# Where a step's gathers of value blocks stand: ahead of a step, or behind the value products of the step before it

## The chip, the cores and the metric

The kernel runs on one core of one Trainium2 chip. The metric is the device time of one execution in microseconds. A core has TensorE (PE, matrix products; PEld is its loading of weights), VectorE (DVE), ScalarE (ACT), GpSimd (POOL) and SyncE (SP). Each takes its own queue of instructions in the order of the program and waits for the others through semaphores. SyncE only issues transfers here; GpSimd issues the gathers and also subtracts and copies.

## The reference

Two stages for 4 batches, 8 heads, 768 rows and a head width of 64. The first is attention with a block mask: of 24 blocks of 32 keys, a block of queries sees its neighbours, the first and the last block, and three blocks that are drawn at random; the first and the last block of queries see everything.

```
mask = |blk_i - blk_j| <= 1, or either block is the first or the last, or blk_j is sampled for blk_i
attn = softmax(where(mask, q @ k.T / 8, -1e9))        x = attn @ v, heads side by side (B, S, 512)
gate = sigmoid(sum over k of conv_w[k] * x shifted by 4 - k rows)
out  = (gate * (x @ w_val)) @ w_out
```

## The kernel before, in words

**Units and steps.** The blocks of queries are taken two at a time, as a pair: eleven pairs of inner blocks in each batch, and one global pair (first and last block) that counts as two units. `units` holds 52 units, four times 11 + 2. One step of the main loop, `for n in range(N + LAG_V)`, makes the scores of unit n, the value products of unit n - 2 (`LAG_V`) and the transposes of unit n - 1 (`LAG_T`). All work on an engine is chained in program order by `InOrder`, which is why nearly all rows of the profile carry line 83.

**The order within a step, before.** First come the loads: `more_keys()` and `more_values()` in turn until both are far enough ahead. Then scaling of queries, stores, a weight load, `scores` (names `sc`, `s`), the copies of key blocks to `kg` on GpSimd and ACT, `values` (name `av`), and then the transposes (`pt`) in two halves, with `fill` and `prepare` behind each half. `finish` (name `xp`) ends the step.

**Value blocks.** `load_values` fetches what a pair's value products need: on SyncE the two own blocks into `va`, on GpSimd two indirect gathers into `vb`, one for each block of queries. Both have three buffers, which come free when the value products of the pair three earlier are done. `more_values` lets the load for a pair go as soon as the value products that free its buffer have been put in the program, that is at the head of the following step. For the first pair of a batch it also puts the index arithmetic (`indices`) on DVE.

**The second stage.** It is worked off in between, by row tiles of 384 rows, two in a batch. `gates` is convolution and tanh on DVE and ACT (`th`). `split` makes a high part `xh` (ACT) and a low part `xl` (GpSimd, a subtraction). `project` is a generator of which each `fill` takes one call (the digits of `FILLS` tell how many fills a half makes, those of `STEPS` how many times `prepare` goes on). Its first four calls are groups of 12 products into `vp`; with each of them DVE makes `y` of the group before (two buffers), ACT its high part `yh`, and GpSimd, by `second`, its low part `yl` one call later. The next six calls are the halves of three output row blocks `op` of 128 rows, six products each. The first half of a block uses high parts only. The second half makes three low-part products, two high-part ones and one with the last low part; in the first block of a row tile that call, the sixth of ten, is also where the last `yl` is put in GpSimd's queue.

Of the kernel before, what the change touches and what calls it, by code (L numbers as in the profile page):

```python
# [22 lines left out]
CH = 4  # L23
KW = 5
TS = 384
TILES = [[(0, 384), (384, 384)]] * B
PAIRS = [(2 * p + 1, 2 * p + 2) for p in range(NP - 1)]
RING = 4
VRING = 3
# [3 lines left out]
LAG_T, LAG_V = 1, 2  # L33
# [13 lines left out]
FILLS = (  # L47
    "11111210010222221221011022"
    "22111000222222111202211111"
    "02021011111110020111111002"  # L50
    "11211111221001111120020111"
    "1200"
)
# [11 lines left out]
def attention_moe(ctx, tc, qb, kb, v, ve, sampled, w_val, conv_w, w_out, ident_in, slot_in, out):  # L65
# [142 lines left out]
    decoded = set()  # L208
# [25 lines left out]
    for b in range(B):  # L234
        bt = Batch()
# [198 lines left out]
    def values(un):  # L434
        pr = un.pr
        if un.e == 0:
            pr.av = ps_av.tile([128, 2, 2, DV], F32, tag="av", name="av")
        if pr.glob:
            for h in range(2):
                for c in range(6):  # L440
                    pt = un.PT[4 * h + c if c < 4 else 4 + 2 * h + c]
                    for hp in range(HP):
                        cols = slice(BLK * hp, BLK * hp + BLK)
                        hd = 2 * hp + h
                        matmul(
                            pr.av[cols, un.e, h, :], pt[:, cols], pr.bt.vn[:, c, hd * DV : (hd + 1) * DV],
                            start=c == 0, stop=c == 5, tile_position=(0, BLK * hp),
                        )
        else:
            slots = [(a, h, b, (4 * a + 2 * b + h) * DV) for a in range(2) for h in range(2) for b in range(2)]  # L450
            wide = pr.bt.b < WIDE
            if wide:
                for a, h, b, hd in slots:
                    matmul(
                        pr.av[64 * b : 64 * b + 64, a, h, :], un.PT[4 * h + 2 * a][:, 64 * b : 64 * b + 64],
                        pr.va[:, hd : hd + DV], start=a + h == 0, stop=False, tile_position=(0, 64 * b),
                    )
            for a, h, b, hd in slots:
                for c in range(1 if wide else 0, 2):
                    for j in range(2):  # L460
                        rows = slice(64 * b + BLK * j, 64 * b + BLK * j + BLK)
                        vt = pr.vb[:, j, :] if c else pr.va
                        matmul(
                            pr.av[rows, a, h, :], un.PT[4 * h + 2 * a + c][:, rows], vt[:, hd : hd + DV],
                            start=c == 0, stop=a + h == 2 if wide else c == 1, tile_position=(0, rows.start),
                        )
        if un.last:
            rs = three.tile([128, 2, 2, 2], F32, tag="rs", name="rs")
            dve.tensor_scalar_add(rs[:, 0], pr.av[:, :, :, D], 1e-9)
            dve.reciprocal(rs[:, 1], rs[:, 0])  # L470
            pr.x = two.tile([128, 2, 2, D], F32, tag="x", name="x")
            dve.tensor_tensor(
                out=pr.x, in0=pr.av[:, :, :, 0:D], in1=rs[:, 1, :, :, None].to_broadcast([128, 2, 2, D]), op=ALU.mult
            )
# [27 lines left out]
    def gates(m):  # L502

        xT, t, n = m.bt.xT, m.t, m.n
        m.th = two.tile([128, CH, TS], F32, tag="th", name="th")
        acc = [m.th[:, f, 0:n] for f in range(CH)]

        def first(f):
            act.activation(acc[f], xT[:, f, t : t + n], AF.Copy, scale=cw[:, f, 0:1])

        def tanh(f):
            act.activation(acc[f], acc[f], AF.Tanh, scale=0.5)

        first(0)
        yield
        for f in range(CH):
            for k in range(1, KW):
                dve.scalar_tensor_tensor(
                    out=acc[f], in0=xT[:, f, t + k : t + k + n], scalar=cw[:, f, k : k + 1], in1=acc[f],
                    op0=ALU.mult, op1=ALU.add,  # L520
                )
                if k == 1 and f + 1 < CH:
                    first(f + 1)
                if f and k == 2:
                    tanh(f - 1)
                yield
        yield
        tanh(CH - 1)
        m.bt.read.add(("gate", m.t))
        yield  # L530
# [89 lines left out]
    to_gate, to_split, to_project = [], [], []  # L620
# [6 lines left out]
    step = [0]  # L627

    def advance(jobs, after=None):

        m, g = jobs[0]
        try:
            next(g)
        except StopIteration:
            jobs.pop(0)
            if after is not None:
                after(m)

    def queue_rows(bt, t):
        m = Rows()  # L640
        m.bt, (m.t, m.n), m.ready, m.begun = bt, TILES[bt.b][t], [], False
        to_gate.append((m, gates(m)))
        to_split.append((m, split(m)))

# [5 lines left out]
    weights = load_weights()  # L650
    decoding = decode_weights()

    def fill(times=1):
        for _ in range(times):
            if "all" in decoded and to_project and step[0] > max(to_project[0][0].ready):
                advance(to_project)

    def prepare(steps):
        for _ in range(steps):
            if next(decoding, None):  # L660
                continue

            if to_gate and (to_gate[0][0].begun or len(gating) < 2):
                to_gate[0][0].begun = True
                gating.add(id(to_gate[0][0]))
                advance(to_gate, prepared)

        if {CH, CH + 1} <= decoded and len(staged) == 2 * CH and to_split and unread <= {id(to_split[0][0])}:
            advance(to_split, prepared)
# [5 lines left out]
    def freed(k):  # L675

        return units[min(k, N - 1)].pr.seq if k >= 0 else -1

    def more(which, upto, load):
        if at[which] < len(pairs) and pairs[at[which]].seq <= upto:  # L680
            load(pairs[at[which]])
            at[which] += 1
            return True

    def until(which, n, do):
        while at[which] < min(len(pairs), pairs.index(units[min(n, N - 1)].pr) + 1):
            do(pairs[at[which]])
            at[which] += 1
# [7 lines left out]
    for n in range(N + LAG_V):  # L696
        step[0] = n

        def more_keys():
            return more("keys", freed(n - 1) + RING, load_keys)  # L700

        def more_values():
            return more("values", freed(n - LAG_V - 1) + VRING, load_values)

        if n == 0:
            more_keys()
            numbers_first = {eng: list(block_numbers(pairs[0], eng)) for eng in (POOL, ACT)}
            until("scaled", 0, scale)
            indices(0)
            until("copied", 0, copy_keys)  # L710
            more_keys()
            until("copied", 1, copy_keys)
            more_values()
        else:
            while more_keys() or more_values():
                more_values()
        until("scaled", n + (SCALE_AHEAD if n else 1), scale)
        store()
        k = len(staged)
        if k < 2 * CH and n >= WEIGHTS_AT[k] and (k < 4 or k - 4 in decoded):  # L720
            next(weights)

        if n < N:
            scores(units[n])
        if n == 0:
            more_keys()
        until("copied", n + COPY_AHEAD, copy_keys)
        if n == 0:
            while more_keys() or more_values():
                more_values()  # L730
        if 0 <= n - LAG_V < N:
            values(units[n - LAG_V])
        if 0 <= n - LAG_T < N:
            for half, _ in enumerate(transposes(units[n - LAG_T])):
                at_half = 2 * n + min(half, 1)
                fill(int(FILLS[at_half]))
                prepare(int(STEPS[at_half]))
        else:
            fill(1)
            prepare(int(STEPS[2 * n]))  # L740
        if 0 <= n - LAG_V < N and units[n - LAG_V].last:
            pr = units[n - LAG_V].pr
            finish(pr)
            pr.bt.done.add(pr.p)
            for t, (r0, rn) in enumerate(TILES[pr.bt.b]):
                need = {p for p in range(NP - 1) if any(r0 <= i * BLK < r0 + rn for i in PAIRS[p])}
                if r0 == 0 or r0 + rn == S:
                    need.add(-1)
                if t not in pr.bt.queued and need <= pr.bt.done:
                    pr.bt.queued.add(t)  # L750
                    queue_rows(pr.bt, t)
# [53 lines left out]
```

## Time and profile before

| | before |
|---|---|
| median of 3 runs | 403.19 us |
| the runs | 397.3, 403.19, 405.37 us |
| span of the profiled execution, first to last instruction | 371.7 us |
| what lies around it, by the runs shown | 25.6 to 33.7 us |
| TensorE busy | 347.2 us, 93% of the span |
| DVE, ACT, GpSimd busy | 256.9, 253.9, 221.4 us |
| gathers into vb | 88 |

Of the profiled execution the page gives the span and no time of its own; the runs give whole times. Times of the trace count from the start of the span. In the rows, the first number of a timeline is the start, the second the length, xN the number of instructions merged, and the brackets give the idle time of the engine ahead of the row and what ended it.

### The profile page before, as it was taken

The numbers are of one execution on the slowest core, as the hardware profiler recorded it, in microseconds if no ns is written. First come the engines' busy times: TensorE is split into PE (matmuls) and PEld (weight loads), VectorE is DVE, ScalarE is ACT, GpSimd is POOL, SyncE is SP. The second block draws the span as 40 slices with busy tenths as digits, with TensorE's granted clock in tenths as the row PEclk, the third lists the DMA queues.
The fourth block names the chain that finished last, engine by engine and source line by source line (L and its number), as shares of the span: only waits on it lengthen the run. The fifth ranks groups of instructions, "written<-read, shape, count | busy, mean of one in ns | idle before, by whom it ended". The sixth has DMA issues, their size and how long they took to land.

```text
span 371.7 us, 15536 instructions
## 1 busy us (share of the span) xinstructions
PE 347.2 (93%) x6274; PEld 274.2 (74%) x6274; DVE 256.9 (69%) x546; ACT 253.9 (68%) x619; POOL 221.4 (60%) x309
## 2 busy tenths in 40 slices
PE   8889789798969999999999999999999999999895
PEld 7456456565646887797779877888888788888794
DVE  4465659975796779577977867586479848959420
ACT  2887678896788777766677587667667766755221
POOL 1888564988478658655861476658454744525540
PEclk9999989998989999999999999999999999999999
DMA  6999983899984537889798257788862473010202
GB/s 231 301 322 318 324 258 91 281 262 297 342 234 113 151 79 222 243 241 280 185 305 260 71 146 234 208 272 260 247 202 83 134 204 109 21 68 19 82 6 86
DMA packets 52585, 72.37 MB, mean 195 GB/s; under 512 B 6944, under 2 KB 34720, under 8 KB 52512
## 3 DMA queue, kind: packets, MB, share of 16 engines
q1 hardware_dynamic: 44896, 47.69, 42.5%
q0 software_dynamic: 7040, 23.43, 21.0%
q8 instruction: 50, 0.82, 0.9%
q10 hardware_dynamic: 576, 0.24, 0.2%
q14 instruction: 23, 0.19, 0.2%
HBM read 65.05 MB, written 6.29 MB: 192 GB/s over the span
## 4 chain that ended last, share of the span: by engine, by line
PE 71%; DVE 10%; DMA 6%; issue 4%; POOL 4%; ACT 4%; SPq 0%; ACTq 0%; POOLq 0%; DVEq 0%
PE op L83 15%; PE vp L83 15%; PE av L83 13%; PE pt L83 12%; PE sc L83 10%; DVE mx L83 4%; DMA vb<-in_v,idx 4%; PE xp L83 3%; PE s L83 3%; DVE th L83 2%; DMA k<-in_k 2%; ACT ptr L83 1%; POOL yl L83 1%; POOL vb L83 1%; DVE words L83 1%
## 5 line engine op out<-in xcount | busy, mean ns | idle before, releaser
L83 POOL DMA_INDIRECT vb<-in_v,idx x88 | 88.5, 1006 | 48.5 <-PE av L83 24.9
L83 DVE SCALAR_TENSOR_TENSOR th<-xT,cw,th 128x384 f32<-128x384 f32 x128 | 100.8, 796 | 11.8 <-ACT th L83 9.5
L83 ACT ACTIVATE pe<-sc,mx 128x256 f32<-128x256 f32 x176 | 69.2, 479 | 39.0 <-DVE mx L83 38.9
L83 DVE TENSOR_REDUCE mx<-sc 128x2 f32<-128x512 f32 x88 | 56.6, 685 | 42.1 <-PE sc L83 39.7
L83 POOL TENSOR_TENSOR yl<-y,yh 128x384 fp32r<-128x384 f32 x32 | 35.9, 1121 | 59.7 <-ACT yh L83 54.5
L83 ACT COPY ptr<-pt 128x512 f32<-128x512 f32 x112 | 65.1, 603 | 7.7 <-PE pt L83 7.5
L83 POOL COPY kg<-k 128x256 f32<-128x256 f32 (+1 forms) x143 | 51.0, 394 | 8.3 <-DMA k<-in_k 8.2
L83 PE MATMUL sc<-kg,qc 64*32 64x256 f32 x1408 | 52.5, 396 | 2.0 <-ACT pe L83 1.4
L83 PE MATMUL op<-wo,yh 128*128 128x512 f32 x192 | 53.6, 401 | 0.0
L83 PE MATMUL pt<-ident,pe 128*128 128x128 f32 x352 | 52.2, 283 | 0.0
L83 PE MATMUL vp<-xh,wv 128*128 128x384 f32 x256 | 51.3, 341 | 0.0
L83 PEld LDWEIGHTS av<-va,ptr 128*32 128x32 f32 (+1 forms) x1056 | 31.0, 118 | 22.3 <-issue 10.9
L83 PEld LDWEIGHTS pt<-ident,pe 128*128 128x128 f32 x352 | 39.5, 142 | 6.8 <-issue 0.4
L83 PEld LDWEIGHTS vp<-xh,wv 128*128 128x128 f32 x256 | 44.2, 188 | 0.2
L83 PE MATMUL av<-va,ptr 128*32 128x65 f32 (+1 forms) x1056 | 40.4, 226 | 3.2 <-ACT ptr L83 3.1
L83 POOL TENSOR_TENSOR xl<-xT,xh 128x384 fp32r<-128x384 f32 x32 | 36.6, 1149 | 11.0 <-ACT xh L83 10.9
L83 PE MATMUL av<-vb,ptr 128*32 128x65 f32 x1408 | 38.4, 222 | 1.6 <-DMA vb<-in_v,idx 1.4
L83 PEld LDWEIGHTS op<-wo,yh 128*128 128x128 f32 x192 | 34.7, 188 | 6.6
L83 PEld LDWEIGHTS sc<-kg,qc 64*32 64x32 f32 x1408 | 22.9, 109 | 18.3 <-issue 8.2
L83 PE MATMUL op<-wo,yl 128*128 128x512 f32 x96 | 31.8, 412 | 1.6 <-POOL yl L83 1.5
L83 PEld LDWEIGHTS av<-vb,ptr 128*32 128x32 f32 x1408 | 30.2, 110 | 3.6 <-DMA vb<-in_v,idx 2.1
L83 DVE SCALAR_TENSOR_TENSOR y<-th,vp 128x384 f32<-128x384 f32 x32 | 17.6, 549 | 20.6 <-PE vp L83 18.7
(72 smaller groups left out, 453.2 us busy)
## 6 DMA issues: line engine op xcount, KB each, us to landing
kg<-in_k SPq DMA_DIRECT2D x165, 64.0 KB
vn<-in_v SPq DMA_DIRECT2D x12, 520.0 KB
qc<-in_q SPq DMA_DIRECT2D x48, 128.0 KB
k<-in_k SPq DMA_DIRECT2D x12, 512.0 KB
out<-ot SPq DMA_DIRECT2D x23, 256.0 KB
va<-in_v SPq DMA_DIRECT2D x44, 130.0 KB
wst<-in_w_val SPq DMA_DIRECT2D x4, 512.0 KB
wst<-in_w_out SPq DMA_DIRECT2D x4, 512.0 KB
```

The costliest lines, as they stand in the source:

```text
L83: made = getattr(self.eng, name)(*args, **kwargs)
```

## The change

The load of a pair's value blocks is allowed one place earlier: in step n, directly behind the value products that free the buffer, instead of at the head of step n + 1. There is one exception. Where the first half's fills would make a row tile's sixth call, the one with the last low-part products of its first block, the load stays behind that half (behind its fills and its `prepare`). `groups` counts the calls that a row tile has made.

```
+    def may_project():
+        return "all" in decoded and to_project and step[0] > max(to_project[0][0].ready)
+
     def fill(times=1):
         for _ in range(times):
-            if "all" in decoded and to_project and step[0] > max(to_project[0][0].ready):
+            if may_project():
+                to_project[0][0].groups += 1
                 advance(to_project)
+
+    def before_last_low(times):
+
+        return may_project() and to_project[0][0].groups <= CH + 1 < to_project[0][0].groups + times
...
         if 0 <= n - LAG_V < N:
             values(units[n - LAG_V])
+
+        def next_values():
+            while more("values", freed(n - LAG_V) + VRING, load_values):
+                pass
+
+        if n >= LAG_V and not before_last_low(int(FILLS[min(2 * n, len(FILLS) - 1)])):
+            next_values()
         if 0 <= n - LAG_T < N:
             for half, _ in enumerate(transposes(units[n - LAG_T])):
                 at_half = 2 * n + min(half, 1)
                 fill(int(FILLS[at_half]))
                 prepare(int(STEPS[at_half]))
+                if n >= LAG_V:
+                    next_values()
```

`CH` is 4, so `CH + 1` is the number of the sixth call, counted from 0. In `queue_rows` a row tile now starts with `groups` at 0.

## Rows read from the trace of the kernel before

**Rows 1.** Busy time by stage: stretch in us and its length, then busy time and number of instructions for PE, PEld, DVE, ACT and POOL, the granted TensorE clock, the DMA share and GB/s.

```profile
50.00:110.00 60.00, 50.08 (x1195) 35.23 (x1180) 47.88 (x103) 49.08 (x129) 43.97 (x71) 0.96 0.84 247
110.00:331.00 221.00, 220.03 (x4207) 178.79 (x4206) 164.18 (x331) 156.72 (x368) 132.71 (x163) 0.99 0.62 184
```

**Rows 2.** The list of waits: who waited for whom, us in total, times, longest.

```profile
PEld op L83 <- POOL yl L83: 3.2, 4, 1.8
...
PE av L83 <- DMA vb<-in_v,idx: 1.4, 2, 0.9
```

**Rows 3.** Timeline of GpSimd, 56 to 78 us.

```profile
64.22 1.27 POOL L83 TENSOR_TENSOR wv<-words,wv 128x512 fp32r<-128x512 f32 x1 [4.74 <-ACT wv L83]
65.64 0.99 POOL L83 DMA_INDIRECT vb<-in_v,idx  x1
...
75.03 1.27 POOL L83 TENSOR_TENSOR wo<-words,wo 128x512 fp32r<-128x512 f32 x1
76.46 1.02 POOL L83 DMA_INDIRECT vb<-in_v,idx  x1 [0.16 <-PE pt L83]
```

**Rows 4.** The chain of work that ended last, in order of time: start, length in us, what.

```profile
77.78 6.77 DMA vb<-in_v,idx
...
218.46 1.07 PE av L83 x64
```

**Rows 5.** Timeline of TensorE, 79 to 89 us (steps 14 to 16).

```profile
79.35 1.09 PE L83 MATMUL pt<-ident,pe 128*128 128x128 f32 x8
...
80.79 1.12 PE L83 MATMUL sc<-kg,qc 64*32 64x256 f32 x32
...
82.85 0.57 PE L83 MATMUL av<-va,ptr 128*64 128x65 f32 x12 [0.67 <-ACT ptr L83]
...
84.60 0.66 PE L83 MATMUL av<-vb,ptr 128*32 128x65 f32 x30 [0.95 <-DMA vb<-in_v,idx]
...
85.19 1.97 PE L83 MATMUL pt<-ident,pe 128*128 128x128 f32 x8
...
87.51 1.61 PE L83 MATMUL sc<-kg,qc 64*32 64x256 f32 x32
```

**Rows 6.** Busy time in short stretches, columns as in rows 1.

```profile
81.80:85.20 3.40, 1.78 (x57) 1.27 (x49) 1.29 (x2) 3.24 (x10) 3.23 (x7) 1.00 1.05 322
85.20:88.60 3.40, 3.40 (x38) 2.65 (x42) 1.95 (x6) 1.76 (x4) 3.10 (x6) 0.50 1.09 288
...
341.20:344.60 3.40, 2.45 (x11) 1.69 (x9) 3.37 (x5) 2.23 (x6) 3.40 (x3) 1.00 0.01 2
```

**Rows 7.** Timeline of step 24: GpSimd, and the last output product of the call on TensorE.

```profile
137.33 1.13 POOL L83 DMA_INDIRECT vb<-in_v,idx  x1
...
140.42 1.00 POOL L83 TENSOR_TENSOR yl<-y,yh 128x384 fp32r<-128x384 f32 x1
...
141.48 0.50 PE L83 MATMUL op<-wo,yl 128*128 128x512 f32 x1 [0.20 <-POOL yl L83]
```

**Rows 8.** Timeline of TensorE in step 35: the last value products, then the two calls of output products.

```profile
212.74 0.32 PE L83 MATMUL av<-vb,ptr 128*32 128x65 f32 x8
...
213.40 1.63 PE L83 MATMUL op<-wo,yh 128*128 128x512 f32 x6
...
215.22 0.95 PE L83 MATMUL op<-wo,yl 128*128 128x512 f32 x3
...
216.72 0.50 PE L83 MATMUL op<-wo,yl 128*128 128x512 f32 x1
```

**Rows 9.** Timeline of GpSimd in step 35 and at the head of step 36.

```profile
211.34 1.01 POOL L83 TENSOR_TENSOR yl<-y,yh 128x384 fp32r<-128x384 f32 x1 [4.52 <-ACT yh L83]
212.30 1.01 POOL L83 TENSOR_TENSOR xl<-xT,xh 128x384 fp32r<-128x384 f32 x1
215.37 1.29 POOL L83 TENSOR_TENSOR yl<-y,yh 128x384 fp32r<-128x384 f32 x1 [2.07 <-ACT yh L83]
...
218.11 0.99 POOL L83 DMA_INDIRECT vb<-in_v,idx  x1 [0.16 <-issue]
219.41 0.95 POOL L83 DMA_INDIRECT vb<-in_v,idx  x1 [0.30 <-issue]
```

**Rows 10.** Timeline around 165 us: the last value products of step 28 on TensorE, and the first gather behind them on GpSimd.

```profile
164.59 0.32 PE L83 MATMUL av<-vb,ptr 128*32 128x65 f32 x8
...
165.25 0.99 POOL L83 DMA_INDIRECT vb<-in_v,idx  x1 [2.46 <-PE av L83]
```

**Rows 11.** Timeline of step 40: a yl on GpSimd, the last value products on TensorE, and the y on DVE that takes the buffer which this yl reads.

```profile
241.18 1.01 POOL L83 TENSOR_TENSOR yl<-y,yh 128x384 fp32r<-128x384 f32 x1
...
242.35 0.32 PE L83 MATMUL av<-vb,ptr 128*32 128x65 f32 x8
...
245.46 0.55 DVE L83 SCALAR_TENSOR_TENSOR y<-th,vp 128x384 f32<-128x384 f32 x1 [1.20 <-PE vp L83]
```

**Rows 12.** Timeline: one scaling of a query block on DVE, the load of a query block on SyncE, and the scaling of that block on DVE.

```profile
217.01 1.10 DVE L83 TENSOR_SCALAR qc<-qc 128x256 f32<-128x256 f32 x1
...
232.03 0.38 SPq L83 DMA_DIRECT2D qc<-in_q  x1
...
238.42 0.29 DVE L83 TENSOR_SCALAR qc<-qc 128x256 f32<-128x256 f32 x1
```

**Rows 13.** All gathers: duration on GpSimd in ns (shortest, median, longest), first and last start in us, number.

```profile
L83 POOL DMA_INDIRECT vb<-in_v,idx x88: 942/966/1317, 12.3 to 313.5; - x88
```

More of the change, by code (lines that the diff above doesn't have):

```diff
@@ L640, in queue_rows @@
         m = Rows()
-        m.bt, (m.t, m.n), m.ready, m.begun = bt, TILES[bt.b][t], [], False
+        m.bt, (m.t, m.n), m.ready, m.begun, m.groups = bt, TILES[bt.b][t], [], False, 0
         to_gate.append((m, gates(m)))
```

## The prediction

> **What bounds the kernel now.** I read the busy time by stages first [rows 1]. From 110 to 331 us TensorE is busy 220.03 of 221 us, so there is no more than about 1 us to gain there, while whatever makes TensorE wait is lost in full. Before that, from 50 to 110 us, it is busy 50.08 of 60 us: this is where earlier gathers could pay. The list of waits comes next [rows 2]: TensorE waits for gathered value blocks 1.4 us in all, and its weight loads wait 3.2 us for yl. So the worth of the change to TensorE is small on either side. Then I went along the GpSimd queue step by step (a step begins with its scores; V is the end of its value products) and looked for places where a gather is late, or where yl is only just in time.
>
> **The change, part by part.** It adds and removes no operation. The two gathers that stood at the head of step n+1, with the load of va on SyncE and three times a run the index arithmetic on DVE, move to behind the value products of step n. What they are moved past: on GpSimd the yl and xl subtractions of step n, on SyncE the stores and key loads of step n+1, on DVE the gate work of step n. The new wait is GpSimd's and SyncE's wait for V, earlier in their queues; behind it are those subtractions, for which TensorE waits, and those loads.
>
> *Gathers that come too late now.* At 84.60 us TensorE waits 0.95 us for a gather [rows 5]; the chain of waits leads to the transfer that began at 77.78 and took 6.77 us [rows 4]. Its pair stood in the GpSimd queue behind a weight subtraction at 75.03, and the whole queue was late, because GpSimd had idled 4.74 us ahead of 64.22 for ACT [rows 3]. After the change the pair of 65.64 (2.25 us by the pair in [rows 9]) goes into that idle time, and the pair of 76.46 also passes its 1.27 us subtraction: some 3.5 us earlier, against 0.95 wanted. **-0.95**; the other end is 0, if the transfer lands no earlier because the DMA engines are full there (share 1.05 and 1.09) [rows 6].
>
> *The clock behind that wait.* TensorE idled 0.67 and 0.95 us [rows 5] in a stretch where it was busy 1.78 of 3.4 us, and in the next stretch its granted clock is 0.50, the 1.2 GHz level [rows 6]. There 8 transposes take 1.97 us and the scores 1.61, where they took 1.09 and 1.12 a step before at full clock [rows 5]: 0.88 + 0.49, and about 0.2 for the two small transposes between them, is 1.6 us. Without the 0.95 the stretch would be busy 2.7 of 3.4 us, more than the 2.45 in the tail where the clock stayed at 1.00 [rows 6]. I take **-1.6**; the other end is 0, if the clock falls a little later instead.
>
> *Step 24 (TensorE at 137 to 144 us).* A gather at 137.33 stood ahead of yl at 140.42, and the last low-part product began at 141.48 after 0.20 us idle [rows 7]. The gathers go to step 23. Step 24 is one that the new test protects, so its own new gathers stay behind this yl. **-0.2**, between 0 and the whole 0.2.
>
> *Step 35 (TensorE at 211 to 217 us).* Here the two fills of the step are one call in each half: the first half makes the call of six high products (213.40), the second the call of three low, two high and one low product (215.22 to 216.72) [rows 8]. The test looks at the first half alone, finds no such call there and lets the gathers go ahead. V is 212.74 + 0.32 = 213.06. Where a gather waits for value products alone it begins 0.3 us after them (164.59 + 0.32, then 165.25) [rows 10], which gives 213.4. Two gathers with their gap take 219.41 + 0.95 - 218.11 = 2.25 us [rows 9], to 215.6. Only then come the yl that ran at 211.34 (1.01, to 216.6), the xl that ran at 212.30 (1.01, to 217.6) and the last yl, now at 215.37 (1.29; 1.01 at its best, to 218.65) [rows 9]. The third low product wants the first of these at about 215.7, the last product the second at 216.72 [rows 8]. So TensorE idles about 0.9 us, makes its two high products, and idles some 1.2 us more; the last product starts at 218.65 and not at 216.72: **+1.95**. Nothing covers it, since all that TensorE has next is behind this product. From below +1.0, if the xl is not ahead of the last yl in time; from above +2.2, with the 1.29.
>
> *The clock behind that.* About 2.1 us idle within 3 us is more than the 1.62 ahead of the fall at 85; the tail's 0.95 of 3.4 lowered nothing [rows 5, 6]. By the nearer row, the first, it falls: **+1.6**, the price from above; other end 0.
>
> *The other row tiles.* In four of them a yl at an early fill gets behind V and two gathers. Step 40: the yl of 241.18 moves to 242.35 + 0.32 + 0.3 + 2.25 = 245.2, ends at 246.2, and DVE's y at 245.46, which reuses the buffer that this yl reads, waits until then: 0.8 us [rows 11]. Behind it on DVE are gate sums; TensorE still has 12 projection products, four transposes, 6 output products and the next scores before it wants the next maxima. I take 0; upper end 0.8 us for each of four, were DVE's lateness passed on in full.
>
> *SyncE.* The load of va now waits for V ahead of the next step's query and key loads, where these waited for the end of the scores: later by a step's value products, 1.07 us [rows 4]. The shortest time from a query load to the scaling that needs it is 232.03 to 238.42 [rows 12], 6.4 us, and keys are loaded three steps ahead of their scores. **0**; a late query would stop DVE for the excess, once, 1 us at most. The index arithmetic, on 24 columns, is smaller than the 0.29 us of the scaling of 256 [rows 12], and delays DVE's gate work by that: 0.
>
> *The ports.* DVE's scaling of a query took 1.10 us at 217.01, beside a GpSimd subtraction, and 0.29 at 238.42 [rows 12]: the two engines can hold each other up. All 88 gathers lie between 942 and 1317 ns [rows 13], so a gather costs at most 0.35 us more by it, and I take 0. The Trainium skill (SBUF — State Buffer, Who interferes with whom) says that the second of DVE and GpSimd to ask for their common ports is fully blocked until the first is done; the same page gives about 3100 ns for a GpSimd-issued DMA beside a DVE copy, 620 ns alone. An estimate from that page would make step 35 some 4 us longer; the trace of before has no gather like it.
>
> **Sum:** -0.95 - 1.6 - 0.2 + 1.95 + 1.6 = +0.8 us. Of its execution the profile gives the span alone, 371.7 us; the runs shown have 397.3 to 405.37 with a median of 403.19, so 25.6 to 33.7 us lie around the span, and nothing in the change touches them. Forecast: 403.2 + 0.8 = **404.0 us**. That is no change: 2%, or 8 us, is about what a measurement of this kernel can tell from none.
>
> **Rivals.** (a) *Slower:* the early gain does not come, because the full DMA engines land the gathers no earlier, and step 35 loses its 3.55: 406.7. If also DVE passes on 0.8 us in four row tiles, 409.9. It decides whether in step 35 the last yl ends after 216.72, and whether DMA at 75 to 88 us is bound by its load rather than by the issue. For it: TensorE has no slack after 110 us [rows 1], and the DMA share [rows 6]. Against it: GpSimd idles 4.74 us ahead of 64.22, so the gathers can go out before the full stretch [rows 3]. (b) *Faster:* the early 2.75 are gained (with step 24), and step 35 loses 1.0 without a fall of the clock: 401.4; if it lost nothing, 400.4. For it: the clock did not fall in the tail [rows 6]. Against: GpSimd takes its queue in the program's order. (c) *The move does nothing:* GpSimd waits for V anyhow, as ahead of 165.25 [rows 10], so that the gathers start where they did: 403.2. Against: the pair of 218.11 starts 5 us behind its V [rows 8, 9]. (d) *The ports:* gathers beside DVE's work take longer at step 35 by 0.35 us each and hold up DVE too: +0.7, 404.7. By the page of the Trainium skill named above it would be about 408.
>
> **How the numbers follow.** Forecast 404.0: 0.55. (a) 406.7: 0.15, its far end 409.9: 0.05. (b) 0.15. (c) 0.07. (d) 0.03. The range reaches from (b)'s 400.4, less 2 us for the spread of the runs, to (a)'s 406.7 and the 2.2 us by which the highest run lies above the median: 398 to 409. Faster by over 2% means below 395.1; no case gives that, and I leave it 0.04 for runs like the 397.3 on top of (b). Slower by over 2% means above 411.3: (a)'s far end with a slow run, 0.08. Within 2%: 0.88.
>
> **What would show it.** Right: no wait for a gathered block at step 15 and a granted clock of 1.00 there; gathers 0.3 us behind V wherever GpSimd is free; in step 35 yl behind two gathers, TensorE idle ahead of its third low and its last low product; no such wait in steps 24, 30 and 41. Wrong: step 35 without that idle time (the forecast is then too high by up to 3.55), a fall of the clock elsewhere, DVE's y waiting for yl with TensorE idle behind late maxima, or a query load that DVE waits for.

## The result, and the profile after

| | before | after |
|---|---|---|
| median | 404.28 us (4 runs, 397.3 to 407.31) | 384.95 us (4 runs, 384.27 to 385.59) |
| ratio of the times | 1 | 0.9644, 95% interval 0.9592 to 0.9696 |
| span of the profiled execution | 371.7 us | 383.8 us |
| time of that execution less its span | not given | 385.59 - 383.8 = 1.8 us |

The change made the kernel 3.0 to 4.1% faster; the forecast was no change. The two records say the opposite of the times: the span after is 12 us *longer* than the one shown of before. That is the riddle of this case, and its solution is that the record of before and its times belong to different conditions. The same kernel before ran at 401 to 406 us in four sittings and at 373 to 376 us in five (a sitting is a set of runs made together on one chip), never in between; within a sitting all its runs stay at one level, apart from one of 1780.98 us. Medians are of all runs, ratios of the fast runs alone, those within 1.5% of the fastest of their kernel. The record shown of before, with a span of 371.7 us, is one of the lower level; its times are of the upper.

The page of after and its list of waits (who waited for whom: us in total, times, longest):

```profile
span 383.8 us, 15523 instructions
...
PE 350.1 (91%) x6274; PEld 275.0 (72%) x6274; DVE 264.1 (69%) x546; ACT 253.6 (66%) x619; POOL 221.0 (58%) x309
```

```profile
PE av L83 <- issue: 4.6, 9, 1.0
PE op L83 <- POOL yl L83: 3.3, 3, 1.3
...
PE s L83 <- ACT xT L83: 1.9, 2, 1.7
```

The wait for gathered blocks of [rows 2] is no longer in the list. A record of this kind could not name it, as it gives no landing time for gathers (see the last section), but the list of r3, which is of the lower level, has none either. TensorE's waits for yl have grown from 1.5 us to 3.3: 2.00 us of them belong to step 35, which came out as forecast, the rest to the tail, which has them in before too. New are waits put down to "issue" inside the value products, of which the list that [rows 2] is taken from has none. TensorE in step 35, after (rows 8 answer to it):

```profile
220.17 0.72 PE L83 MATMUL op<-wo,yl 128*128 128x512 f32 x2
221.95 0.50 PE L83 MATMUL op<-wo,yl 128*128 128x512 f32 x1 [1.06 <-POOL yl L83]
222.29 0.63 PE L83 MATMUL op<-wo,yh 128*128 128x512 f32 x2
223.85 0.50 PE L83 MATMUL op<-wo,yl 128*128 128x512 f32 x1 [0.94 <-POOL yl L83]
```

GpSimd in the same step (rows 9 answer to it):

```profile
219.64 1.23 POOL L83 DMA_INDIRECT vb<-in_v,idx  x1 [0.30 <-issue]
220.90 1.00 POOL L83 TENSOR_TENSOR yl<-y,yh 128x384 fp32r<-128x384 f32 x1
221.84 1.01 POOL L83 TENSOR_TENSOR xl<-xT,xh 128x384 fp32r<-128x384 f32 x1
222.81 0.98 POOL L83 TENSOR_TENSOR yl<-y,yh 128x384 fp32r<-128x384 f32 x1
```

The gather, then yl, xl and the last yl: TensorE waits for the first yl and the last one. And the clock behind it (stretch, length, busy time of PE, PEld, DVE, ACT, POOL, granted clock, DMA share, GB/s):

```profile
224.33:227.74 3.41, 3.41 (x83) 1.92 (x82) 2.36 (x4) 1.56 (x4) 1.52 (x3) 0.50 0.18 53
```

### The profile page after: what moved, and what is told of

Read it like the earlier page. It is cut to its first block, busy times and chain, and to the rows that moved or that the text cites. A ratio compares the mean times of both kernels' runs of the same rounds, so it can differ in the third digit from the quotient of the medians.

```text
span 383.8 us, 15523 instructions
## 1 busy us (share of the span) xinstructions
PE 350.1 (91%) x6274; PEld 275.0 (72%) x6274; DVE 264.1 (69%) x546; ACT 253.6 (66%) x619; POOL 221.0 (58%) x309
## 4 chain that ended last, share of the span: by engine, by line
PE 65%; DVE 16%; ACT 7%; issue 6%; POOL 3%; DMA 1%; ACTq 1%; DVEq 0%
PE av L83 13%; PE op L83 13%; PE vp L83 13%; PE sc L83 11%; PE pt L83 9%; DVE th L83 7%; DVE mx L83 4%; PE xp L83 3%; PE s L83 3%; ACT pe L83 2%; ACT ptr L83 1%; DVE x L83 1%; POOL vb L83 1%; DMA sb<-in_sampled 1%; ACT kg L83 1%
## 5 line engine op out<-in xcount | busy, mean ns | idle before, releaser
L83 POOL DMA_INDIRECT vb<-in_v,idx x88 | 89.7, 1019 | 91.4 <-PE av L83 66.1
L83 DVE SCALAR_TENSOR_TENSOR th<-xT,cw,th 128x384 f32<-128x384 f32 x128 | 111.0, 875 | 11.8 <-ACT th L83 9.5
L83 POOL TENSOR_TENSOR yl<-y,yh 128x384 fp32r<-128x384 f32 x32 | 34.7, 1091 | 38.6 <-ACT yh L83 38.2
L83 POOL COPY kg<-k 128x256 f32<-128x256 f32 (+1 forms) x143 | 52.2, 402 | 8.1 <-DMA k<-in_k 8.0
L83 PE MATMUL av<-va,ptr 128*32 128x65 f32 (+1 forms) x1056 | 41.3, 229 | 4.5 <-ACT ptr L83 2.2
L83 PE MATMUL av<-vb,ptr 128*32 128x65 f32 x1408 | 40.0, 225 | 2.6 <-issue 2.4
L83 POOL TENSOR_TENSOR xl<-xT,xh 128x384 fp32r<-128x384 f32 x32 | 35.4, 1111 | 6.1 <-ACT xh L83 5.9
L83 PEld LDWEIGHTS av<-vb,ptr 128*32 128x32 f32 x1408 | 31.1, 112 | 4.8 <-issue 3.2
```

What stands on the lines that cost most here:

```text
L83: made = getattr(self.eng, name)(*args, **kwargs)
```

## The experiments

**Is the profiled execution of before a typical one? (r1)** The kernel before, unchanged.

> The kernel before, unchanged. In the changed kernel's runs the whole time is 1.8 us above the span (385.59 against 383.8); in the kernel before, the median of 404.28 is 32.6 us above the profiled span of 371.7. Theory A: the profiled execution of the kernel before was an unusually quick one, and its usual executions have a span about 2 us below their time, near 402 us; then this run shows a span of 395 to 406 us, a time 1 to 3 us above it, and in the trace waits of 20 us or more that the first profile does not have. Theory B: the span is 372 us in every execution and 30 us lie around it; then this run shows a span of 370 to 374 us and a time of 397 to 407 us.

374.15 us (372.47 to 377.29), beside 374.04 for its twin; span 371.2, so 1.8 us lie around it. On this chip it simply ran 30 us faster than in the first runs. The "25.6 to 33.7 us around the span" of the prediction do not exist.

**The step that the test misses (r2).** The exception looks at both halves of a step, and holds the gathers back behind the first half if the second makes the sixth call:

```
-        if n >= LAG_V and not before_last_low(int(FILLS[min(2 * n, len(FILLS) - 1)])):
+        if n >= LAG_V and not before_last_low(sum(int(x) for x in FILLS[2 * n : 2 * n + 2])):
...
-                if n >= LAG_V:
+                if n >= LAG_V and not (half == 0 and before_last_low(int(FILLS[2 * n + 1]))):
```

> The changed kernel, with the exception made for both halves of a step: only step 35's GpSimd queue differs from it (two gathers go behind two yl and two xl). If the idle 2.0 us at step 35 and the fall of the clock behind it are what the changed kernel loses there, this run shows no idle time at step 35, a granted clock of 1.00 in steps 36 and 37, and a time 3 to 4 us below the changed kernel's 384.95: 381 to 382 us. Rival: the lost time comes back elsewhere, since the gathers of step 35 then land later; the time stays within 1 us of 384.95.

377.03 against 374.04, ratio 1.0122 (1.0057 to 1.0187). Step 35 has no idle time and a clock of 1.00; from the start of step 35 to that of step 38 it takes 17.86 us (before 17.34, after 21.04). So the mechanism of step 35 is as predicted, and undoing it does not bring the time below that of before. The times of the expectation miss, as this sitting was at the other level.

**The change again, and its two halves apart (r3 to r5).** `load_values` split into the own rows (SyncE, va) and the gathered rows (GpSimd, vb); r4 moves the gathers alone, r5 the own rows alone.

> The changed kernel, unchanged, beside new runs of the kernel before. The kernel before took 404 us in the first set of runs and 374 in the second, with a span 1.8 us below its time in both the profile (371.7) and the second set. Theory A: where the kernel before takes 374, the change costs time (the changed kernel with step 35 protected took 377.03 there), and this run is 378 to 382 us, a loss of 4 to 8; its gain in the first set comes from a condition in which the kernel before is slow. Theory B: the change gains the same 4% everywhere, which would be 358 to 362 us beside 374, with step 35's loss offset by something the two first profiles don't show.

377.87 against 375.93, ratio 1.0061 (1.0025 to 1.0098): on this chip, where before needs 376, the changed kernel is about 2 us *slower*.

> Only the gathers on GpSimd (with their index arithmetic) go behind the value products, as in the changed kernel; the loads of va on SyncE stay at the head of the next step, as in the kernel before. If GpSimd's queue is what the change is about, gain or loss, this run is within 1 us of the changed kernel. If SyncE's earlier wait (va ahead of the key loads) costs something, this run is quicker than the changed kernel by that, 1 to 3 us.

381.26, ratio 1.0162 (1.0088 to 1.0236); TensorE waits once for 3.0 us for va.

> The other part alone: the loads of va on SyncE go behind the value products, the gathers stay at the head of the next step. If GpSimd's queue is what matters, this run is within 1 us of the kernel before, with no idle time at step 35. If SyncE's order matters, it moves by the 1 to 3 us that the gathers alone do not show.

380.12, ratio 1.0162 (1.0069 to 1.0255); TensorE waits three times, 3.8 us in all, for gathered blocks. Neither part gains where before is at its lower level. Both miss their expectations: they are 3.4 and 2.3 us above r3, and why a part costs more than the whole is open.

**Another chip (r6 to r8).** The change, the wider exception of r2, and the change without any exception (`if n >= LAG_V:`).

> The changed kernel once more, in a third set, beside the kernel before. Theory A (the gain of the first set belongs to a condition in which the kernel before runs at 397 to 407 us): the result depends on what the kernel before takes in this set; at 372 to 378 the changed kernel is 0 to 6 us slower, at about 400 it is quicker and at 380 to 386. Theory B (it is always quicker): 358 to 362 us beside 374.

384.73, and before beside it 403.78 (402.89 to 406.54): ratio 0.9526 (0.9481 to 0.9571). This is the first result again.

> The changed kernel with the exception made for both halves of a step, now beside the changed kernel itself. From the traces, TensorE's way from the scores of step 35 to those of step 38 took 21.05 us in the changed kernel and 17.86 with this protection: if nothing hides that, this run is 2 to 4 us quicker than the changed kernel. Rival: it is not, because the spread of the stage before 120 us (2 to 4 us from execution to execution) covers it.

384.85, ratio 0.9508 (0.9448 to 0.9568): no difference from r6 that can be measured, and not the 2 to 4 us expected. The records say why: in r7 step 35 has no idle time, but the gathers held back (223.82 and 225.12 us) run beside the value products of step 36, which take 3.39 us instead of 1.14, and in r6 the idle time of step 35 had no fall of the clock behind it. Steps 35 to 38 take 19.52 us in r7 and 19.50 in r6.

> The changed kernel without its exception: in steps 24, 30 and 41 too, the gathers go ahead of the last yl. By the working of step 35, each of the three loses about 2 us of idle time at the last low-part product, and 1.5 us more where the clock falls behind it: 6 to 10 us slower than the changed kernel. Rival: yl was early enough in these steps, and the exception is worth nothing (within 1 us).

395.15, ratio 0.9774 (0.9717 to 0.983), 10.4 us more than r6. Steps 24, 30 and 41 now have what step 35 has, with 1.88 to 1.89 us idle in each; TensorE at step 24:

```profile
148.77 0.60 PE L83 MATMUL op<-wo,yl 128*128 128x512 f32 x1 [1.88 <-POOL yl L83]
```

and its clock is 0.50 in 149.03 to 152.44. The exception is worth its place: half of the gain hangs on it.

**The kernel before recorded at the upper level, and which part carries the gain there (r9 to r11).** r9 is before, r10 as r4, r11 as r5.

> The kernel before, unchanged, to see it recorded on a chip where it needs about 404. What is to be read is where the some 30 us lie that it needs less on the two other chips, and whether they stand behind waits of the value products for gathered or own rows (tags vb and va). Theory G (gathers that land late: before starts each gather a half step later than changed, and the smallest time from landing to first use was 0.1 to 2 us around steps 13 to 18): on a chip with 404 the record shows TensorE's value products waiting on vb at several places, together some 5 to 15 us, each followed by about 3.4 us at a granted clock of 0.5. Theory P (something that has nothing to do with the values: waits for a transposed or scaled tile, or for instructions): the vb and va waits stay under 2 us in all, and the idle time stands elsewhere. On a chip where before needs about 374 the record is as before's: vb waits under 2 us, and the question stays open.

402.12; span 399.3. Waits of TensorE in this record:

```profile
PE av L83 <- issue: 13.0, 33, 1.1
PE xp L83 <- DVE x L83: 8.5, 6, 2.6
```

and in r1, the same program at the lower level:

```profile
PE xp L83 <- DVE x L83: 1.5, 3, 0.7
...
PE av L83 <- issue: 0.8, 1, 0.8
```

> Only the gathers start early; the own rows' loads stay where the kernel before has them. On a chip where before needs about 404: theory G says 385 to 390, as the whole change; theory P in the form that the own rows' loads on SyncE carry the gain says 400 or more. On a chip where before needs about 374: 378 to 381 as in the first run of it.

386.38, ratio 0.9667 (0.9566 to 0.9768).

> Only the own rows' loads start early; the gathers stay where the kernel before has them. On a chip where before needs about 404: theory G says 398 to 406, no gain that can be told; if the own rows' loads carry the gain it says 385 to 390. On a chip where before needs about 374: 377 to 381 as in the first run of it.

405.34, ratio 1.0145 (1.0076 to 1.0213). The gathers carry all of the gain, the own rows none. Theory G was right in that, and wrong in its reason: the waits are not for gathered rows, since the products that read va stand still as well as those that read vb, and the gather beside them fetches rows for a later pair. The value products stand still in the middle of a group, in which nothing is waited for that the profile shows. Step 36 of r9, TensorE:

```profile
239.77 0.34 PE L83 MATMUL av<-va,ptr 128*32 128x65 f32 x8
239.91 0.40 PE L83 MATMUL av<-vb,ptr 128*32 128x65 f32 x8
...
240.77 0.26 PE L83 MATMUL av<-va,ptr 128*32 128x65 f32 x2 [0.45 <-issue]
...
241.50 0.22 PE L83 MATMUL av<-vb,ptr 128*32 128x65 f32 x1 [0.40 <-issue]
...
242.24 0.29 PE L83 MATMUL av<-vb,ptr 128*32 128x65 f32 x3 [0.41 <-issue]
...
242.74 0.30 PE L83 MATMUL av<-vb,ptr 128*32 128x65 f32 x6
```

GpSimd at that time:

```profile
239.48 0.99 POOL L83 DMA_INDIRECT vb<-in_v,idx  x1 [0.15 <-issue]
240.78 0.95 POOL L83 DMA_INDIRECT vb<-in_v,idx  x1 [0.30 <-issue]
```

The same 64 products in r1, TensorE and then GpSimd:

```profile
215.59 0.33 PE L83 MATMUL av<-va,ptr 128*32 128x65 f32 x8
...
216.41 0.32 PE L83 MATMUL av<-vb,ptr 128*32 128x65 f32 x8
```

```profile
215.30 0.99 POOL L83 DMA_INDIRECT vb<-in_v,idx  x1
216.59 0.95 POOL L83 DMA_INDIRECT vb<-in_v,idx  x1 [0.30 <-issue]
```

The gathers lie 0.29 us ahead of the products in both. In r1 the group takes 1.14 us, in r9 3.28, and its products come in small bursts 0.73 us apart. I measured all 52 groups of value products in each record, from the first product's start to the last one's end, against the shortest of their size (1.14 us for 64, 1.28 for 48, 1.57 for 96). In r9, of the 32 groups from the 21st on, 9 have a gather's issue beside them: they are longer by 1.12 to 2.14 us, 13.2 us together. The other 23 are longer by 0.1 us together. In r1, 8 groups with a gather and 2 touched by one have 0.7 us together. Over all 52 groups, r9 has 29.8 us of excess and r1 8.9; waits for ptr inside a group and a lower clock are in both sums. TensorE's idle time ahead of the transposes of x (xp), whatever the list puts it down to, is 10.0 us in r9 and 4.1 in r1. Together that is 20.9 + 5.9 = 26.8 of the 28.1 us between the two spans.

The three longest waits for x, 6.7 us together, do not come from stretched groups: in the groups ahead of them a gather's issue begins only in the last 0.3 us. Step 11 of r9: the end of the value products, the two gathers, the first work of DVE on those products, and the transposes of x:

```profile
70.50 0.67 PE L83 MATMUL av<-vb,ptr 128*32 128x65 f32 x32
70.96 0.99 POOL L83 DMA_INDIRECT vb<-in_v,idx  x1
72.26 0.94 POOL L83 DMA_INDIRECT vb<-in_v,idx  x1 [0.30 <-issue]
73.81 0.16 DVE L83 TENSOR_SCALAR rs<-av 128x4 f32<-128x4 f32 x1 [3.14 <-remote]
74.80 0.41 PE L83 MATMUL xp<-ident,x 128*128 128x128 f32 x2 [2.61 <-DVE x L83]
```

(The "remote" in the brackets says little, as semaphore events are missing from this record.) The group takes 2.19 us, as in r1 (2.17), but DVE, idle, takes up its result 2.65 us later, 0.61 us behind the second gather's issue. In r1, with a gather's issue at 65.42, it starts 0.14 us behind the products:

```profile
65.75 0.16 DVE L83 TENSOR_SCALAR rs<-av 128x4 f32<-128x4 f32 x1 [0.62 <-PE av L83]
```

Wherever DVE was idle before this work, it starts in r9 1.3 to 2.7 us behind the products in six places with a gather's issue there, and at most 0.08 us behind them in four without; in r1 it is at most 0.14 us in all nine. So at the upper level the issue also goes with a late start of DVE on TensorE's results. The records show this side by side; no experiment was made for it alone.

Neither the transfers nor GpSimd's other work does it. Value products in three stretches of r9 (stretch, length, busy time of these products and their number, granted clock, DMA share, GB/s):

```profile
239.70:243.00 3.30, 1.98 (x64) 1.00 0.46 101
254.20:255.60 1.40, 1.14 (x64) 1.00 0.94 102
266.50:268.00 1.50, 1.14 (x64) 1.00 1.04 367
```

The last two have the DMA engines full and are not stretched; the last also has a yl on GpSimd beside it.

**Taking the gathers away, or moving them later (r12 to r15).** In before, each gather replaced: in r12 by `pool.memset(pr.vb[:, j, :], 1.0)`, in r13 by `sp.dma_start(pr.vb[:, j, :], v[r0 : r0 + 128, :])`. r14: the changed kernel with `SP_VALUES = ((1,), (), (), ())`. r15: before, with the gathers behind the *next* step's value products.

> The kernel before with every gather replaced by a GpSimd write of ones into the same half of the same buffer: it leaves out the gathered rows, their traffic and the issue of the indirect transfers; GpSimd stays in its place in the order, with the same waits. Theory I (on the chips where before needs about 404, a value product that runs beside the issue of a gather on GpSimd is stretched; the issue does it): on such a chip 372 to 386, no group of value products over 1.7 us after step 20. Theory W (GpSimd's work on the buffer, of whatever kind, does it): 395 or more, and the groups beside a write are stretched to 2.2 us or more. On a chip where before needs about 374: 366 to 376 by both, which tells nothing apart.

363.26 against 373.59, ratio 0.9735 (0.9663 to 0.9808).

> The kernel before with every gather replaced by one plain load on SyncE of 128 rows that lie together, of the same size, into the same half of the same buffer, at the same place in the order: it leaves out the choice of the rows. The traffic stays, the issue on GpSimd goes. On a chip where before needs about 404: theory I says 372 to 386 with no stretched group of value products after step 20; theory T (the traffic of the gathers stretches them, on its way through memory) says 393 or more with 5 or more stretched groups. On a chip where before needs about 374: 368 to 380 by both.

389.3, ratio 1.0452 (1.0372 to 1.0533), with 6.8 us of waits for va and 4.5 for vb: the additional loads on SyncE make its own rows late.

> The changed kernel with the second half of the gathered rows of the first batch loaded block by block on SyncE (a table of the kernel allows it), so that one gather of two goes in steps 0 to 13. A candidate for a better version on a chip where before needs about 404: there theory I says 378 to 384, as the changed kernel still has some 8 groups of value products stretched by 0.5 to 2.6 us in the steps up to 18, and half of their gathers go; the rival is that SyncE's four more loads per pair come late and it needs 385 to 395. On a chip where before needs about 374: 375 to 385.

393.43, ratio 1.0562 (1.0481 to 1.0643): the block loads hold up SyncE, and TensorE's scores stand for 10.2 us. No better version.

> The kernel before with each gather one half step LATER: it waits for the same value products as in before, and stands behind the next step's value products instead of ahead of them. On a chip where before needs about 404: theory I says 384 to 395, since the nine stretched groups after step 20 (13.2 us in the record) lose the gather beside them, though every gather lands later than in before; the rival, that what the change brings there is the earlier start, says 404 or more. On a chip where before needs about 374: 374 to 384, from waits for rows that land late.

378.19, ratio 1.0119 (1.0075 to 1.0162). Its premise was wrong too: eleven groups after the 20th still have a gather beside them, those of the step after. This sitting was at the lower level, so that these four do not tell the theories apart. r12 comes out 3 us below its range; r13 and r14 lie above theirs, with the waits just named.

**A gather put beside the value products, and GpSimd writes as the control (r16 to r18).** In the changed kernel, from step 21 on:

```
+        if marked(units.index(un)):
+            dve.tensor_copy(extra[:, 0:1], sc[0][:, 0, 0:1])
...
+        if n % 2:
+            for _ in range(3):
+                pool.memset(extra, 1.0)
+            return
+        pool.indirect_dma_start(out=extra, ..., in_=v.rearrange("n (e d) -> (n e) d", e=2), ...)
```

(r16 takes n % 3, with nothing in every third step, and the last scores as the start.)

> The changed kernel with extra work on GpSimd beside the value products of steps from 21 on, behind a small VectorE copy of the step's scores that times it: in one step of three an extra gather of 128 half rows into a tile that nobody reads, in the next three GpSimd writes of ones into that tile, in the third nothing. On a chip where before needs about 404 theory I says: every group of value products that has an extra gather beside it in its first microsecond takes 1 us or more longer than 1.14 (64 products) or 1.28 (48), those beside writes or beside nothing stay within 0.3; the whole kernel 394 to 410 instead of 385. Theory W (GpSimd's work of any kind): the groups beside writes are stretched as much. Theory O (something of the earlier order of before, not the gather): neither, and 385 to 390. On a chip where before needs about 374: no group is stretched by over 0.4 in any step, and 378 to 386.

380.07, ratio 1.0208 (1.0124 to 1.0293), lower level: groups with the extra gather take at most 1.29 us.

> As r16, with the extra work in every step from 21 on that has no global pair in it or in its value products, started by the first half of the step's scores: an extra gather of 128 half rows in even steps, three GpSimd writes in odd ones. Where the kernel before, run beside it, needs about 404, theory I says: groups of value products with an extra gather beside them in their first 0.8 us take 1.0 to 2.3 us longer than 1.14, those with writes beside them stay within 0.2; the whole kernel 395 to 415. Theory W: both are stretched. Theory O (only the order of before matters): neither, and 385 to 392. Where before needs about 374: none is stretched by over 0.4, and 379 to 388.

385.79, ratio 1.0272 (1.021 to 1.0335), lower level again: with the extra gather from 0.66 us on, four groups of 64 products take 1.23, 1.24, 1.25 and 1.31 us.

> The kernel of r17 once more. Where the kernel before, run beside it, needs about 404, theory I says: groups of value products with a gather's issue beside them in their first 0.8 us take 1.0 to 2.3 us longer than 1.14, those with writes beside them stay within 0.2; the whole kernel 395 to 415. Theory W: both are stretched. Theory O: neither, and 385 to 392. Where before needs about 374: as r17, 381 to 389, and no group longer than 1.14 by over 0.4.

399.4, before beside it 406.44 (397.01 to 411.54), ratio 0.998 (0.9919 to 1.0041): upper level, and the same program as r17. Five groups of 64 with the extra gather from 0.66 us on take 2.22, 2.24, 2.32, 2.33 and 2.45 us. All seven of 64 products with GpSimd writes beside them take 1.14 us. TensorE beside an extra gather of r18, and GpSimd:

```profile
235.44 0.44 PE L83 MATMUL av<-va,ptr 128*32 128x65 f32 x8
...
236.15 0.32 PE L83 MATMUL av<-vb,ptr 128*32 128x65 f32 x8
236.27 0.63 PE L83 MATMUL av<-va,ptr 128*32 128x65 f32 x3
...
237.46 0.32 PE L83 MATMUL av<-va,ptr 128*32 128x65 f32 x4 [0.39 <-issue]
237.59 0.30 PE L83 MATMUL av<-vb,ptr 128*32 128x65 f32 x4
```

```profile
225.67 1.06 POOL L83 MEMSET extra<- 128x260 f32 x3 [5.54 <-DVE extra L83]
...
236.10 0.99 POOL L83 DMA_INDIRECT extra<-in_v,idx  x1 [1.73 <-DVE extra L83]
```

Up to the gather's start the products come at their usual pace, eight in 0.11 to 0.22 us; from then on in drops, until 0.37 us behind its end. Beside the writes of 225.67 the group of 225.28 takes 1.14 us. Two groups that the extra gather meets near their end are not stretched: one of 64 with it from 0.88 us on takes 1.30, one of 48 with it from 0.77 us on takes 1.42, against 1.44 in r17. And the drops are over before this gather moves anything. All engines in the stretch that holds them (stretch, length, busy time of PE, PEld, DVE, ACT, POOL, granted clock, DMA share, GB/s):

```profile
236.10:237.50 1.40, 0.87 (x36) 0.54 (x25) 0.93 (x2) 0.98 (x3) 0.99 (x1) 1.00 0.00 0
```

No transfer runs there, so the drops are not its traffic (theory T, left untested by r13). This settles it: at the upper level the *issue* of a gather on GpSimd stretches value products beside it, at the lower level it lengthens them by 0.1 to 0.2 us (r17), and GpSimd's writes do not at either.

## Why the prediction was wrong

**The step that failed** is "25.6 to 33.7 us lie around the span, and nothing in the change touches them". r1, r3, r6 and r9 have 1.8 us there. The difference was not around the span but in it: the times shown had been run under a condition that the record shown did not have. What the change touches most, gathers beside value products, costs 13.2 us and more in the one condition and next to nothing in the other, so no row of the record of before had it. I could have seen that something did not fit: 26 to 34 us outside the first and last instruction is 6 to 8% of a kernel, and I took it for a constant instead of a contradiction. No rival covered it.

**The term that was sized at nothing** follows from it: a gather that is moved was weighed by its lateness, by GpSimd's queue and by the ports it shares with DVE, never by what it does, while it is being issued, to TensorE and to DVE's start on TensorE's results. At the upper level the change takes the issue off most of the value products: excess of the 52 groups 29.8 us in r9, 14.3 in r6; idle time ahead of the transposes of x 10.0 and 4.5. That is 15.5 + 5.5 = 21.0 us won, and the spans differ by 399.3 - 382.3 = 17.0; 4.0 us are given back. By stages (start of a step to start of a step, TensorE, us; the stages left out differ by 1.2 us at most):

| steps | before, lower (r1) | before, upper (r9) | after, lower (r3) | after, upper (r6) |
|---|---|---|---|---|
| 0 to 10 | 56.85 | 63.05 | 59.56 | 61.80 |
| 10 to 18 | 36.25 | 45.77 | 35.65 | 38.38 |
| 18 to 22 | 23.41 | 26.11 | 23.65 | 23.28 |
| 24 to 31 | 43.96 | 48.58 | 43.43 | 43.72 |
| 31 to 35 | 29.67 | 30.82 | 30.75 | 30.74 |
| 35 to 38 | 17.34 | 21.05 | 21.05 | 19.50 |
| 38 to 41 | 21.17 | 21.17 | 21.27 | 22.52 |
| 46 to 54 | 46.50 | 46.33 | 47.21 | 47.23 |

**The other steps**, against the record of after. *The late gather at step 15 and the clock behind it* (-0.95, -1.6): the wait is gone and the clock is 1.00 from 50 to 110 us. At the lower level steps 10 to 18 gain 0.6 us from r1 to r3, not 2.55: r1, the same program as before, does not have that wait at step 15, and in r3 the clock falls at 76.0 us, at the end of a wait of 1.77 us for ptr. The record shown of before takes 37.91 us there, 1.7 more than r1, so one execution differs from another by most of what was forecast. Steps 0 to 10 are 2.7 us longer in r3; where that comes from is open. *Step 24* (-0.2): 6.72 us before, 6.26 after, -0.46. *Step 35* (+1.95 and +1.6): 1.06 + 0.94 = 2.00 us idle, then the clock at 0.50; steps 35 to 38 take 21.04 us where the record before has 17.34, +3.70 for 3.55. That the clock fell was not certain: in r6 the same 2.00 us idle had no fall behind it. *Other row tiles* (0): DVE's y now waits for yl four times, 8.3 us in all, once and 1.9 us before. The list puts 0.3 us of TensorE's idle time down to y; what the rest cost it was not measured by itself. *SyncE* (0): wrong. DVE waits once for a late query block, 1.2 us after, 1.6 in r6 and 2.4 in r3, where 1 us at most was given. *Not foreseen:* 1.69 us idle at step 31 for xT from ACT.

At the lower level, the condition of the record on which it was worked out, the sum of +0.8 us stands beside 376 x 0.0061 = +2.3 us (0.9 to 3.7): the right sign, and small. But step 35 alone has its +3.7, and r2, without it, is no faster than r3, so the sum was near for partly other reasons. Rival (a) was that step, and at the upper level its idle time is paid too; rival (d), the ports, asked the right question, what a gather does to its neighbours, of the wrong neighbour. The longest gather of after takes 1460 ns (1317 in [rows 13]), beside DVE's SCALAR_TENSOR_TENSOR. The Trainium skill (SBUF — State Buffer, A bandwidth-pool intuition that's wrong (but worth ruling out)) gives about 3100 ns for one beside a DVE tensor_copy; no run here shows a gather that long.

No version beat both kernels at both levels: before is best at the lower (374 against 377 to 378), the change at the upper (385 against 404).

## What to carry to other kernels

Hold the span of the profiled execution against the times before working out anything: where they differ by more than the couple of us that lie around a span, the record is not of the executions that were timed, and no sum made on it holds for them. When a GpSimd-issued transfer is moved, look also at what TensorE does *while it is issued*: in one of the two conditions seen here one or two gathers' issues of 1 us each cost the value products beside them 1.1 to 2.1 us, in the other next to nothing. And repeat a surprising result on another chip before explaining it.

## What the runs showed of the hardware

**Two levels of one program.** 374 (chip 15), 376 (8), 374 (2), 374 (12) and 373 (11); 404 (the first runs), 404 (6), 401 (12) and 406 (0). Chip 12 is in both lists, so if a number names one chip, it is not a property of the chip alone. What sets it is open. The durations of single instructions are the same at both (r9 and r1: scores 390 and 384 ns, maxima 685 and 684), and the gathers land no later at the upper level (by their packets 4.1 and 4.6 us after the start of their issue, medians).

**A mark in the record.** In the eight records of the upper level the list of transfers gives no landing time for the gathers. r9, then r1:

```profile
vb<-in_v,idx POOLq DMA_INDIRECT x88
```

```profile
vb<-in_v,idx POOLq DMA_INDIRECT x88, 4.7
```

That alone is no mark, as r2 and r4, of the lower level, have none either. The better one is the semaphore events (updates of the counters by which engines release each other), which the records of the upper level lack in part: 6,867 in r9 against 8,540 in r1. Nearly all that are missing lie within the issue of the gathers (740 against 2,220, in 88 and 90 us); outside there are 6,127 and 6,320. The shown record of before has 8,523, that of after 6,679, r17 8,747 and r18 6,531. In all eight records of the upper level 740 to 866 events lie within the issue of gathers, in the ten of the lower level that have gathers 1,998 to 2,428. So here the level of a record can be told from itself.

**What may lie behind it** was not tested. The groups that are stretched are those with the densest instructions, 64 products and 64 weight loads in 1.14 us, where scores have 32 and 32 in 1.09; in r9, scores, transposes and output products beside a gather's issue keep their durations (1.09 us for 32 scores and for 8 transposes, 1.63 for six output products). The stretch, the late start of DVE and the missing events have the same place and the same condition. The Trainium skill (Perfetto Trace Analysis, DMA Instruction — SWDGE (GPSIMD)) says that the interval shown for such a transfer is the time in which its descriptors are generated, not that in which data moves; r1 agrees, with about 1.0 us of issue and 4.7 us to the landing. The Trainium skill (NOTIFIC — the notification-queue block, Overflow: three behaviours, one of which stalls the engine) says that the block which writes the records of an execution holds its producers back rather than lose a record inside it. That could make the stretch a price of recording, though it would not explain by itself why events are missing. All timed executions listed with a span and a clock, which are all but those of before in the first runs, seem to have been recorded, and no run here shows one without.
